# Two transfers instead of five for the sketch matrices, placed behind the first keys, and a new instruction sequence, in an attention and token-mixing kernel

## The chip, the cores and the metric

The kernel runs on one core of a Trainium2 chip. The metric is the device time of one execution in microseconds (us); the median of several runs counts. The core's engines run side by side, each through its own list of instructions: TensorE (PE, matrix products), VectorE (DVE), ScalarE (ACT), GpSimd (POOL) and SyncE (SP), which here only issues DMA transfers. An instruction waits until the data it reads is there and the buffer it writes is free.

## What is computed

```python
def phi(x):                                   # S1, S2: (8, 32)
    a = np.einsum('rd,bhsd->bhsr', S1, x)
    b = np.einsum('rd,bhsd->bhsr', S2, x)
    return np.einsum('bhsi,bhsj->bhsij', a, b).reshape(*x.shape[:-1], r * r)
q_p, k_p = phi(q), phi(k)                     # q, k, v: (4, 4, 1088, 32) float32
kv  = np.einsum('bhsf,bhsd->bhfd', k_p, v)
num = np.einsum('bhsf,bhfd->bhsd', q_p, kv)
den = np.einsum('bhsf,bhf->bhs', q_p, k_p.sum(axis=2))[..., None] + 1e-06
x = num / den                                 # then heads side by side: (4, 1088, 128)
...
theta = x @ w_theta
zr, zi = x * np.cos(theta), x * np.sin(theta)
y = einsum('ts,bsd->btd', w_tok_r, zr) + einsum('ts,bsd->btd', w_tok_i, zi)   # 1088 x 1088 each
u = x + y
out = u + np.maximum(u @ w_ch, 0.0)
```

S1, S2 and the weights are float64 in the inputs; q, k and v are float32. The denominator can be small, so sums over keys and queries are kept in several words of rounded parts.

## The kernel before

A 64-bit number arrives as two 32-bit words and is turned into float32 on the chip: ACT makes one word into a float, DVE shifts and joins the other. The kernel calls this path `wide`. It is taken for the sketch matrices S1, S2 (tile `st`, unpacked to `sp`), for the square weights (`w_sq`: w_theta and w_ch, unpacked to `w`) and for the 17 row blocks of the two token matrices (`w_tok`, raw tiles of class `zs`, unpacked into tiles of class `big`).

The stages are these.

1. For each of the four batches keys, queries and values are loaded (`load`, L677, 576 KB each, SP). ACT squares the keys and sums them (L702), PE sums over partitions, and DVE derives a rounding step (`key_step`, first DVE operation on `sm`) and rounds the keys into `hf`. PE forms the key sums from rounded part and remainder.
2. The sketch matrices are unpacked (ACT L471, then DVE shifts and masks, then ACT L483), scaled by a power of two (L495, then ACT L525 to L527) and split in rounded words (`s0`, first DVE operation `s<-sm`).
3. PE transposes keys, forms sketched features, and DVE multiplies them to outer products; PE sums these with the values (`kfeatures`).
4. Three "chains" (batch 0, batch 1, batches 2 and 3) carry the key sums through the sketch; DVE takes their norms (L918) and cuts them in words.
5. Queries get the same treatment (`query_scale` L1006, `query_slices`), then numerators and denominators (`levels`, L1071), theta, cosine and sine on ACT, and the products with x into tiles of class `zs`.
6. The token mix multiplies by the 17 row blocks (`mix_row`), for batches 0 and 1 directly, for batches 2 and 3 by a scheme of seven quarter products instead of eight (`winograd`). It needs sums and differences of quarter matrices; three sets of these are made by DMA transfers that add into their target (`aadd`, L1331, issued by POOL). Such adding transfers also join u = x + y for batches 0 and 1 (L398).
7. The channel product, ReLU, a transpose and the stores (L1286, SP).

No scheduler decides the order. Every piece of work is recorded as an operation with engine, buffers and a duration for planning; the list `ORDER` (1012 numbers) at the top of the file gives the order in which all operations are issued, for all engines together. `Layout.lay` walks that list, plans a start time for each operation from the durations and some constants (`START`: the time at which each engine begins; `ADD_FLY3`: the flight of an adding transfer), and with these picks which buffer of its class each tile gets. `Layout.issue` then emits the instructions in the list's order. Where the plan leaves a gap on PE, it puts in fill matmuls on a zero tile (`spin`, L435), whose result nobody reads. So on each engine the order is the list's; the planned times change only buffer numbers and the number of fills.

The helper lines L384 to L404 record almost every DVE, POOL and PE instruction, so that a line alone does not tell the operation; tile names do.

SP's queue begins with keys of batch 0, w_sq, the sketch transfers, keys of batch 1, queries of batch 0. The sketch transfers are made by `read_heads` (L452 to L457): S1 and S2 side by side, 32 partitions of 128 bytes, are read four times, once for each head's group of 32 partitions, two of them by ACT and two by SP; then SP reads S2 once more in another layout (8 partitions of 256 bytes, into columns 16 to 47 of `st`). A memset of `st` (L463) comes ahead of all, on DVE. On ACT the first Square of keys (L702) comes before the sketch unpack (L471).

Of the kernel before, what the change touches and what calls it, by code (L numbers as in the profile page):

```python
# [21 lines left out]
P = 128  # L22
# [4 lines left out]
TINY = 2.0**-60  # L27
UP = 256.0
ORDER = """
# [37 lines left out]
"""  # L67
WARM = 0
FILL = 5.0
# [13 lines left out]
UDMA = (True, True, False, False)  # L83
ADD_FLY = 2.85
ADD_FLY2 = 1.05 / 384
ADD_FLY3 = 1.6
QFIX = 2.006
NFIX = 1.002

# [16 lines left out]
class Layout:  # L106


    START = {"P": 1.3, "V": 0.8, "A": 1.0, "G": 1.3, "S": 0.9}
    ISSUE = 0.47  # L110
    LAT = {"P": 0.2, "V": 0.04, "A": 0.04, "G": 0.06, "S": 0.10}
    SAME = {"P": 0.0, "V": 0.035, "A": 0.035, "G": 0.05, "S": 0.0}
# [94 lines left out]
    def lay(self):  # L207
# [4 lines left out]
        slots = {c: [[0.0, None, i] for i in range(n)] for c, n in self.classes.items()}  # L212
        free = dict(self.START)
        channel = self.FIRST
# [105 lines left out]
def kernel(  # L320
# [12 lines left out]
    B, _, NC, H, D = q.shape  # L333
    S, DM = out.shape[1], out.shape[2]
    R = s_2.shape[0]
# [34 lines left out]
    op, buf = L.op, L.buf  # L370
# [4 lines left out]
    V, A, G, T, SY = nc.vector, nc.scalar, nc.gpsimd, nc.tensor, nc.sync  # L375

    def fixed(shape, dt, name):
        b = Buf(None, shape, dt, name)
        n = math.prod(shape) * WORD[dt]
        b.ap = view(const.tile([P, (n + 3) // 4], F32, tag=name, name=name), shape, dt)  # L380
        return b
# [4 lines left out]
    def ts(o, a, s1, op0, s2=None, op1=None, eng=None):  # L386
        kw = {} if op1 is None else {"op1": op1}
        (eng or V).tensor_scalar(out=o, in0=a, scalar1=s1, scalar2=s2, op0=op0, **kw)  # L388
# [59 lines left out]
    NS = 2 * R + D  # L448
    sp = fixed((2, NS), F32, "sp")
    wide = s_t.dtype != F32  # L450

    def read_heads(E, i0, i1):  # L452
        dst = st() if wide else sp()[:, 0]
        for i in range(i0, i1):
            E.dma_start(dst[i * D:(i + 1) * D, 0:2 * R], s_t.rearrange("d t r -> d (t r)"))
        if i1 == H:
            E.dma_start(dst[0:R, 2 * R:NS], s_2)  # L457

    if wide:
        st = fixed((NS,), I64, "st")  # L460
        y = fixed((NS,), I32, "sy")
        z = fixed((NS,), I32, "sz")
        op("V", 0.1, lambda: V.memset(st().bitcast(F32), 0.0), [st], [])  # L463
        op("A", 0.48 * 2, lambda: read_heads(A, 0, 2), [(st, 0)], [], fly=2.7)
        op("S", 0.5, lambda: read_heads(SY, 2, H), [(st, 1)], [], lk=3)

        def words():
            w = st().bitcast(I32).rearrange("p (n t) -> p n t", t=2)
            return w[:, :, 0], w[:, :, 1]

        op("A", 0.25, lambda: A.activation(sp()[:, 0], words()[1].bitcast(F32), AF.Prelu, scale=2.0**-112,  # L471
                                           alpha=-(2.0**32)), [(sp, 0)], [st])

        def unpack():
            wl = words()[0]
            x = sp()[:, 0].bitcast(I32)
            ts(x, x, 3, ALU.logical_shift_left)
            stt(x, wl, 29, x, ALU.logical_shift_right, ALU.bitwise_or)
            ts(y(), x, -(1 << 23), ALU.bitwise_and)
            ts(z(), wl, 0x1FFFFFFF, ALU.bitwise_and)  # L480

        op("V", 0.85, unpack, [(sp, 0), y, z], [st], lk=2)
        op("A", 0.25, lambda: A.activation(sp()[:, 1], z(), AF.Copy, scale=2.0**-52), [(sp, 1)], [z])  # L483
        vop(NS, lambda: tt(V, sp()[:, 1], sp()[:, 1], y().bitcast(F32), ALU.mult), [(sp, 1)], [y])
    else:
        op("V", 0.2, lambda: V.memset(sp(), 0.0), [sp], [])
        op("A", 0.4 * H + 0.4, lambda: read_heads(A, 0, H), [(sp, 0)], [], fly=2.0)

    def powers(mfn, m, n, name):

# [6 lines left out]
        def inv():  # L497
# [16 lines left out]
                                    op=ALU.max, apply_absolute_value=True), [m2], [(sp, 0)])  # L514
# [787 lines left out]
    def winograd():  # L1302
# [25 lines left out]
        def aadd(name, dst, x):  # L1328
            at("ac", name)
            for i in range(NF):  # L1330
                op("G", 1.05, lambda i=i: G.dma_start(dst[0](i), x[0](i), accum_op=ALU.add), [dst[1](i)], [x[1](i)],  # L1331
                   chan=ADD_FLY3)

# [170 lines left out]
```

## Time and profile before

| what | value |
|---|---|
| time, median of 3 runs (lowest, highest) | 223.31 us (223.21, 223.4) |
| profiled execution: time, span | 223.25 us, 221.4 us |
| granted clock of PE | 1.00 in all stretches read |
| DMA moved | 40.19 MB, mean 182 GB/s |
| DMA share, 10 to 50 us | 1.02 to 1.04 |
| L404 PE, `ps<-big,zs` (token mix) | x366, 102.4 us busy |
| L435 PE, `ps<-idle` (fills) | x40, 10.9 us busy |

The span runs from the first to the last instruction that the profile records; 1.8 us of the execution lie around it. "Busy" is the time in which an engine works on an instruction; an engine that is not the bottleneck may be idle at no cost. The chain of waits follows the work that ended last back to the start, at each step to whatever released it. A DMA share of 1.0 means that all 16 DMA engines are occupied. `[2.29 <-DMA big<-k_l]` behind an instruction says that its engine stood idle for 2.29 us before it and what ended that. DVE's first five instructions of the sketch unpack start at 7.12, 7.33, 7.58, 7.68 and 7.77 us, and its first rounding of the sketch (`s<-sm`) at 12.33 us.

### The profile page before, as it was taken

To read this page: it belongs to the slowest core of one execution; us is meant where nothing else is said; L and a number is where in the kernel's file an instruction comes from. 1 tells how busy PE (TensorE), PEld (TensorE's weight loads), DVE (VectorE), ACT (ScalarE), POOL (GpSimd) and SP (SyncE) were. 2 spreads that over 40 slices of the span, in tenths; PEclk is the share of its full clock that TensorE was granted. 3 is DMA by queue.
4 is the path that set the end of the run, shared out by engine and by line. 5 is a ranking of instruction groups with operands and counts; after the bars stand their busy time and mean duration, and the time that the engine had idled before them with its cause. 6 is when DMAs were issued, how large, how long until landed. Compare 5 with 4: busy or idle time off the path is not lost.

```text
span 221.4 us, 5134 instructions
## 1 busy us (share of the span) xinstructions
PE 212.4 (96%) x2067; PEld 160.3 (72%) x2067; DVE 167.2 (76%) x360; ACT 115.5 (52%) x237; POOL 47.4 (21%) x81
## 2 busy tenths in 40 slices
PE   7998999899998999999999999999999999999993
PEld 3796888697765756686666685778787888688782
DVE  2999889999999999999999949961798551043741
ACT  4889489988798889769640232586820000000000
POOL 1365751104000000100400090000552337101000
PEclk9999999999999999999999999999999999999999
DMA  6999999993509016948950089020498199983373
GB/s 184 367 410 341 393 411 375 414 360 150 204 16 366 25 42 242 385 154 302 338 103 0 0 134 170 3 39 1 69 179 152 33 171 158 169 122 56 47 116 57
DMA packets 27047, 40.19 MB, mean 182 GB/s; under 512 B 18320, under 2 KB 19344, under 8 KB 24848
## 3 DMA queue, kind: packets, MB, share of 16 engines
q1 hardware_dynamic: 22176, 30.29, 40.2%
q0 software_dynamic: 4752, 9.57, 24.2%
q8 instruction: 16, 0.26, 0.4%
q14 instruction: 7, 0.06, 0.1%
q10 hardware_dynamic: 96, 0.01, 0.0%
HBM read 28.07 MB, written 2.23 MB: 137 GB/s over the span
## 4 chain that ended last, share of the span: by engine, by line
PE 78%; DVE 12%; DMA 5%; SPq 2%; issue 1%; ACT 1%; POOL 0%; DVEq 0%; POOLq 0%
PE ps L404 68%; PE ps L435 4%; DMA zs<-big 3%; DVE g L384 2%; DVE lv L384 2%; PE ps L795 2%; DMA out<-g 2%; PE ps L1158 2%; SPq L1286 2%; PE ps L1191 1%; DVE big L384 1%; PE ps L1038 1%; DVE sm L384 1%; DVE big L388 1%; DVE big L391 1%
## 5 line engine op out<-in xcount | busy, mean ns | idle before, releaser
L404 PE MATMUL ps<-big,zs 128*128 128x384 f32 (+4 forms) x366 | 102.4, 426 | 0.6 <-DVE big L384 0.4
L404 PEld LDWEIGHTS ps<-big,zs 128*128 128x128 f32 x366 | 65.5, 190 | 27.2 <-issue 1.3
L1270 ACT COPY g<-ps 128x384 f32<-128x384 f32 (+1 forms) x6 | 2.6, 464 | 51.2 <-PE ps L404 51.2
L652 ACT ACTIVATE big<-zs 128x1088 int32<-128x1088 uint32 (+1 forms) x18 | 21.2, 1182 | 1.2 <-DMA zs<-w_tok 1.2
L384 DVE CUSTOM_DVE_ANT_0 big<-big,big 128x2176 uint16<-128x2176 uint16 x17 | 21.7, 1285 | 0.1
L650 ACT ACTIVATE big<-zs 128x1088 f32<-128x1088 f32 x17 | 20.6, 1220 | 1.6 <-DMA zs<-w_tok 0.8
L1331 POOL DMA_DIRECT2D big<-zs x8 | 7.9, 1026 | 34.1 <-DVE g L391 23.7
L391 DVE SCALAR_TENSOR_TENSOR big<-ps,even,big 128x256 f32<-128x256 f32 (+1 forms) x10 | 4.9, 498 | 13.5 <-PE ps L404 13.4
L384 DVE TENSOR_TENSOR zs<-ps,g 128x768 f32<-128x768 f32 (+2 forms) x20 | 12.4, 628 | 2.9 <-PE ps L1191 1.4
L404 PE MATMUL ps<-mf,big 128*128 128x96 f32 x72 | 14.3, 295 | 0.0
L398 POOL DMA_DIRECT2D g<-big x6 | 7.1, 1589 | 30.2 <-ACT g L1270 30.2
L404 PE MATMUL ps<-big,big 128*32 128x32 f32 (+2 forms) x320 | 12.9, 219 | 0.0
L388 DVE TENSOR_SCALAR big<-big 128x1088 int32<-128x1088 int32 x17 | 11.9, 720 | 0.4 <-ACT big L650 0.4
L435 PE MATMUL ps<-idle 128*128 128x384 bf16 x40 | 10.9, 406 | 1.3 <-POOL idle L437 1.3
L404 PEld LDWEIGHTS <-hf 128*32 128x32 bf16 (+1 forms) x252 | 10.5, 99 | 2.2 <-issue 1.2
L404 PEld LDWEIGHTS ps<-big,big 128*32 128x32 f32 (+1 forms) x320 | 9.9, 117 | 2.7 <-issue 0.9
L388 POOL TENSOR_SCALAR mf<-mv 128x32 f32<-128x32 f16 (+1 forms) x3 | 1.0, 341 | 49.7 <-DVE mv L388 49.7
L404 PE MATMUL ps<-w,big 128*128 128x128 f32 x76 | 10.9, 279 | 0.8 <-ACT g L1298 0.8
L404 PEld LDWEIGHTS ps<-w,big 128*128 128x128 f32 x76 | 9.9, 191 | 2.0 <-ACT g L1298 1.2
L384 DVE TENSOR_TENSOR g<-lv 128x768 f32<-128x768 f32 x12 | 11.1, 949 | 0.2
L404 PEld LDWEIGHTS ps<-mf,big 128*128 128x128 f32 x72 | 10.9, 191 | 0.1
L404 PE MATMUL ps<-mv,hf 128*128 128x96 f16 x108 | 10.6, 206 | 0.3 <-ACT big L810 0.3
(199 smaller groups left out, 396.2 us busy)
## 6 DMA issues: line engine op xcount, KB each, us to landing
zs<-w_tok SPq DMA_DIRECT2D x17, 1088.0 KB, 6.6
big<-k_l SPq DMA_DIRECT2D x7, 576.0 KB, 6.6
big<-q_l SPq DMA_DIRECT2D x4, 576.0 KB, 12.9
big<-v_l SPq DMA_DIRECT2D x4, 576.0 KB, 13.7
big<-big POOLq DMA_DIRECT2D x8, 272.0 KB, 5.8
big<-zs POOLq DMA_DIRECT2D x8, 272.0 KB, 4.4
zs<-big POOLq DMA_DIRECT2D x8, 272.0 KB, 5.5
big<-hf POOLq DMA_DIRECT2D x3, 576.0 KB, 10.2
```

Source lines behind the costliest of these rows:

```text
L384: eng.tensor_tensor(out=o, in0=a, in1=b, op=f)
L388: (eng or V).tensor_scalar(out=o, in0=a, scalar1=s1, scalar2=s2, op0=op0, **kw)
L391: (eng or V).scalar_tensor_tensor(out=o, in0=a, scalar=s, in1=b, op0=op0, op1=op1)
L398: op("G", 1.05, lambda: G.dma_start(dst(), src(), accum_op=ALU.add), w, r, chan=chan)
L404: T.matmul(o, lhs, rhs, start=start, stop=stop, skip_group_check=True)
L435: T.matmul(nowhere(), idle()[:, 0:P], idle(), start=True, stop=True, skip_group_check=True)
L650: op("A", 0.22 + n * 0.0009, lambda: A.activation(dfn(), words_of(raw(), n)[1].bitcast(F32), AF.Prelu, scale=2.0**-112, alpha=-(2.0**32)), ...
L652: op("A", 0.22 + n * 0.0009, lambda: A.activation(stp(), words_of(raw(), n)[0].bitcast(U32), AF.Copy, scale=2.0**-29), [stp], [raw])
L795: T.transpose(tr()[:, i * P:(i + 1) * P], kx()[:, g * GC + i].rearrange("p h d -> p (h d)"), ident())
L1158: T.transpose(tr()[:, i * P:(i + 1) * P], qp()[:, i * H + 2 * n:i * H + 2 * n + 2].rearrange("p h i j -> p (h i j)"), ident())
L1286: SY.dma_start(out[b, t0 - o:t0 + w, f * SQ:(f + 1) * SQ].rearrange("(c j) i -> j c i", j=SQ), ot()[f * SQ:(f + 1) * SQ, :o + w].rearrange ...
L1331: op("G", 1.05, lambda i=i: G.dma_start(dst[0](i), x[0](i), accum_op=ALU.add), [dst[1](i)], [x[1](i)], chan=ADD_FLY3)
```

## The change

- The four transfers of S1 and S2 side by side become one, whose source is read four times over (`partition_broadcast`), into all 128 partitions. That transfer and the one of S2 are both issued by SP. ACT issues none. One operation of the list goes (1011 numbers).
- The whole of `ORDER` is replaced. In it the two sketch transfers stand right behind the keys of batch 0 on SP, and w_sq behind them; further down SP's loads differ in places. DVE begins with the memset of `st`. On ACT the sketch unpack (old L471) stands before the first Square of keys, on DVE the sketch unpack before the first key step, and the unpacking of w_sq follows later. The order on PE, DVE, ACT and POOL differs in many places up to the token mix and in some behind it. On POOL the last of the adding transfers (old L1331) now stands behind the last join (old L398) instead of before it.
- `START` begins each engine sooner in the plan, and `ADD_FLY3` goes from 1.6 to 1.9. Fills become 39, 13 of them ahead of the first transposes instead of 17.
- The branch for float32 sketch matrices is changed in the same way; these inputs do not take it.

```diff
 ORDER = """
-    0 1 10 11 36 12 3 13 4 5 54 48 108 14 39 58 49 55 51 15 102 59 96 109 56 16 19 60 139 143 61 62 63 64 65 66
...
+    0 1 35 12 5 13 10 11 107 14 53 15 16 18 54 108 57 55 101 19 58 20 47 48 59 17 3 4 60 61 62 63 64 65 66 38 67
...
-ADD_FLY3 = 1.6
+ADD_FLY3 = 1.9
...
-    START = {"P": 1.3, "V": 0.8, "A": 1.0, "G": 1.3, "S": 0.9}
+    START = {"P": 1.05, "V": 0.55, "A": 0.75, "G": 1.05, "S": 0.5}
...
-    def read_heads(E, i0, i1):
+    def read_small():
         dst = st() if wide else sp()[:, 0]
-        for i in range(i0, i1):
-            E.dma_start(dst[i * D:(i + 1) * D, 0:2 * R], s_t.rearrange("d t r -> d (t r)"))
-        if i1 == H:
-            E.dma_start(dst[0:R, 2 * R:NS], s_2)
+        SY.dma_start(dst[:, 0:2 * R], s_t.rearrange("d t r -> d (t r)").partition_broadcast(H))
+        SY.dma_start(dst[0:R, 2 * R:NS], s_2)
...
         op("V", 0.1, lambda: V.memset(st().bitcast(F32), 0.0), [st], [])
-        op("A", 0.48 * 2, lambda: read_heads(A, 0, 2), [(st, 0)], [], fly=2.7)
-        op("S", 0.5, lambda: read_heads(SY, 2, H), [(st, 1)], [], lk=3)
+        op("S", 0.25, read_small, [st], [], lk=3)
```

More of the change, by code (lines that the diff above doesn't have):

```diff
@@ L486 @@
         op("V", 0.2, lambda: V.memset(sp(), 0.0), [sp], [])
-        op("A", 0.4 * H + 0.4, lambda: read_heads(A, 0, H), [(sp, 0)], [], fly=2.0)
+        op("S", 0.25, read_small, [(sp, 0)], [], lk=3)
     def powers(mfn, m, n, name):
```

72 rows, old and new, of the table ORDER are left out of this document.

## The prediction

> **What bounds the kernel now.** I read the busy shares and the chain first, then the chain in order of time.
>
> ```profile
> PE 212.4 (96%) x2067; PEld 160.3 (72%) x2067; DVE 167.2 (76%) x360; ACT 115.5 (52%) x237; POOL 47.4 (21%) x81
> PE 78%; DVE 12%; DMA 5%; SPq 2%; issue 1%; ACT 1%; POOL 0%; DVEq 0%; POOLq 0%
> ...
> 75.55 22.41 PE ps L404 x147
> ...
> 185.16 6.20 DMA zs<-big
> 191.40 21.06 PE ps L404 x90
> ```
>
> TensorE (PE) sets the end. From 75.55 us it is never idle except at 191.40, so whatever makes PE reach that point sooner passes to the end, unless the accumulating DMAs of the last product (zs<-big) then come too late. Before 75 us the limit changes hands, which the busy time by stretch shows (columns: stretch, its length, busy us of PE, PEld, DVE, ACT, POOL, clock, DMA share, GB/s):
>
> ```profile
> 30.00:42.00 12.00, 10.60 (x174) 9.46 (x174) 11.62 (x30) 11.60 (x28) 4.28 (x10) 1.00 1.03 391
> 58.00:70.00 12.00, 11.24 (x152) 7.62 (x151) 11.63 (x20) 11.28 (x24) 0.00 (x0) 1.00 0.40 137
> 100.00:140.00 40.00, 40.00 (x235) 26.51 (x234) 36.22 (x55) 15.47 (x23) 8.87 (x10) 1.00 0.59 144
> ```
>
> At 30-42 and 58-70 us VectorE (DVE) is the fullest (11.62 and 11.63 of 12), ScalarE (ACT) close behind, and the chain runs through DVE there. So the early gain is counted on DVE: how late it is against the work that stands ahead of it. Its waits up to 76 us, whole:
>
> ```profile
> DVE sm L388 <- ACT big L702: 3.4, 1, 3.4
> DVE sm L918 <- PE ps L404: 0.9, 1, 0.9
> DVE halfpi L419 <- PEq L1494: 0.8, 1, 0.8
> DVE big L388 <- ACT lv L1071: 0.5, 1, 0.5
> DVE s L388 <- ACT sm L527: 0.2, 1, 0.2
> ```
>
> Only the 3.4, 0.9, 0.5 and 0.2 can be won. The 3.4 is the place of the change; the timeline there (start, duration, engine, line, what):
>
> ```profile
> 0.73 0.38 SPq L677 DMA_DIRECT2D big<-k_l  x1
> 1.16 0.42 SPq L649 DMA_DIRECT2D zs<-w_sq  x1
> 2.29 0.14 DVE L463 MEMSET st<- 128x96 f32 x1
> 2.46 0.81 SPq L455 DMA_DIRECT2D st<-s_t  x2
> 2.46 0.88 ACTq L455 DMA_DIRECT2D st<-s_t  x2
> 3.31 0.36 SPq L457 DMA_DIRECT2D st<-s  x1
> 3.71 0.36 SPq L677 DMA_DIRECT2D big<-k_l  x1
> 4.50 1.16 ACT L702 ACTIVATE big<-big 128x1152 f32<-128x1152 f32 x1 [2.29 <-DMA big<-k_l]
> 5.79 0.34 DVE L388 TENSOR_SCALAR sm<-sm 128x1 int32<-128x1 int32 x2 [3.36 <-ACT big L702]
> 5.99 0.23 ACT L471 ACTIVATE sp<-st 128x48 f32<-128x48 f32 x1
> ```
>
> The first keys land at 4.48, ACT squares them at once, and DVE, idle for 3.36 us, goes on at 5.79. The sketch unpack (L471 on ACT, then four DVE operations and the reduction, 7.12-7.93) stands behind that.
>
> **The change, part by part.** The sum is made against the profiled execution: 223.25 us, span 221.4 and 1.8 us around it. It lies 0.06 under the median 223.31, so I carry the difference over unchanged.
>
> *Five transfers become two, on SP only.* SP saves one issue of about 0.4, ACT two (0.88). ACT waited 2.29 for the keys afterwards, so its saving is worth nothing. The memset (0.14) leads DVE, inside the 3.36 wait: nothing. On SP the order is now k0, two sketch transfers, w_sq, k1, q0. At 0.4 an issue k1 leaves near 2.4 instead of 3.71, q0 near 2.8 instead of 4.50. The DMA engines are full from 10 to 50 us (share 1.03), so later loads come 1 to 1.5 us sooner. I price that at nothing and use it as the cover for the terms below; without it the loads would eat them.
>
> *The sketch ahead of the first keys.* ACT now does the sketch activation (L471) before the first Square (L702), and DVE's five unpacking operations stand ahead of the key step. Let the sketch land at T. The Square starts at T+0.25 (0.23 for L471 and 0.02), the key step 1.29 later (5.79-4.50). DVE has 1.85 of work ahead of it, 1.19 before: its lateness is T+0.25+1.29-1.85 = T-0.31, against 5.79-1.19 = 4.60. Break-even is T=4.91. T is not in the trace. Lower bound: right with the keys, 4.55. Upper: as late as the last piece now, 5.84. In between: the present pieces, issued at 2.46 to 3.31, land 0.19 to 0.71 behind w_sq (5.13), the load issued ahead of them; the same distance behind the keys gives 4.67 to 5.19. I take 4.85: -0.06. The scale chain behind the unpack starts some 2 us sooner, so the 0.2 wait on L527 goes too. Head: -0.3, bounds -0.6 and +0.7 (T=5.84: +0.93-0.23).
>
> [...]
>
> *The new sequence.* (a) At 25.34 DVE waits 0.86 for PE before the norms (L918). The new order puts 1.7 us of other DVE work ahead of it (a key remainder, a row shift, a rounding). That wait goes if the moved work is ready: its inputs are the loads that now come sooner. -0.7, bounds -0.86 and 0. (b) The 0.46 at 58.02 (DVE on ACT's L1071, itself on PE): PE is sooner, -0.2, bounds -0.46 and 0. (c) Work ahead of the last big DVE step before 70 us (g<-lv at 68.25), summed from the durations of this trace: 59.32 before, 59.55 after: +0.24. (d) New waits: a key-feature product now stands behind an ACT copy that by the same sums comes 0.35 late, and a query Square behind a load near 26.8; +0.2, bounds 0 and +0.7. (e) Fills: 13 spins (L435) lead instead of 17, 39 in all instead of 40. They run while PE has nothing else: nothing.
>
> *The last product.* PE's real work from 75 us on is the same and stands in nearly the same order. The accumulating row additions (L1331) are reordered on POOL. Now PE loses 0.27 at 191.40 (with the rows before it 0.8 of lateness builds up from 184 to 193). In the new order the last row addition stands behind the last join (L398) on POOL: from the end of the matmul group that the join needs, PE has 4 matmuls of 256 columns (0.43 apart) and 11 of 288 (0.485 apart), 7.1 us, until it needs that row. The way takes 0.2 (a reader starts 0.2 behind PE's next group, as at 198.08 and 198.28) + 0.48 (copy, L1270) + 0.29 (its end at 201.27 to the join at 201.56) + 0.86 (the join's issue) = 1.8, then the landing, 4.4 to 5.8 by the medians of the row additions: 6.2 to 7.6. So -0.8 (old lateness gone) to +0.5; I take 0. The constants START and ADD_FLY3 act only through the planner: fills and buffer numbers.
>
> Sum: -0.3-0.7-0.2+0.24+0.2 = -0.76: 222.5 us, span 220.7.
>
> **Rivals.**
> - *The gain is hidden.* ACT has 11.60 of 12 at 30-42 us and DMA is at its limit to 50 us. If ACT or a landing sets that stage, (a) is won and lost again, (b) stays: 0 to -0.2, 223.2. For it: ACT's busy time. Against: DVE stands in the chain there, and the loads come sooner.
> - *The final join blocks POOL.* The slower side. The join's own DMA shares the queue with the row addition, and joins landed in medians of 4.6 (four of 192 KB) and 7.0 us (two of 160 KB). With 7.0 for the row addition the way is 8.8, PE stands 1.7 longer, and -0.76+1.7 = +0.9: 224.2. It decides from a landing of 5.3 us on, and outweighs the gain from about 6.1. For it: POOL takes its instructions in order and L398 waited 12.36 for ACT here. Against: from 192 to 213 us the DMA share is 0.58, against 1.05 before.
> - *The sketch lands late.* 128 pieces of 128 bytes behind the keys, or a repeated source that goes slowly. At T=5.84, +0.7-0.7-0.2+0.24+0.2 = +0.24: 223.5; each 0.1 later adds 0.1, as both the Square and DVE stand behind it, so at 6.5 it is 224.1.
> - *The change doesn't do what it says*: the reading is neutral (T near 4.9) and all comes from the order. The time is then the forecast's, +0.06+0.2 at most: 222.8; it is no case of its own.
> - *Cold PE.* The 17 spins here start about 0.32 us apart up to 6.4 us and then near 0.165; with 13 they end near 5.5, before that step. The first nine key transposes (0.109 each) would then cost double, +1.0 on PE if nothing covered it: 222.5+1.0 = 223.5. Against: DVE, not PE, sets the pace there, and PE still spins after them. [...]
>
> **How the numbers follow.** Forecast, with its own range 221.6 (all low ends but the last product's: -0.6-0.86-0.46+0.24 = -1.7) to 222.9: 0.58. Hidden: 0.15. Final join: 0.14. Late sketch: 0.09. Cold PE: 0.04. The runs shown spread by 0.2 us, so I count 0.2% (0.45 us) as what a measurement can tell. Faster is the forecast, 0.58; within it is the hidden gain and a little of the late sketch and cold PE, 0.17; slower the rest, 0.25. The range for 8 in 10: low end, all low ends with the last product's -0.8, is 220.7; I take 220.8. The high end takes in the final join and half of what the late sketch reaches: 224.5.
>
> **What would show it.** Right: L471 first on ACT, starting before 5.0; DVE's wait for it ends there and the key step starts by 6.3; s (L388 after L527) at or before 12.0; no wait of 0.9 at L918; PE past 75.55's piece some 0.7 sooner. Wrong: a sketch landing after 5.3, DVE or ACT waits over 0.5 us on a load before 50 us, or PE waiting over 0.5 us for zs<-big past 190 us.

## The result, and the profile after

The changed kernel takes 222.31 us (median of 6 runs, 221.82 to 222.86) against 223.36 us (6 runs, 223.15 to 223.57): a ratio of 0.9953, 95% interval 0.9933 to 0.9972. The forecast was 222.5. In three later jobs, on chips where the kernel before took 223.5 to 223.7, it was faster still: 221.90, 221.35 and 221.85 us, ratios 0.9919 (0.9884 to 0.9954), 0.9905 (0.9872 to 0.9939) and 0.9912 (0.9878 to 0.9946). So it is faster by 1.0 to 2.1 us. Some executions of some kernels ran 2 to 5% longer at a lower granted clock (0.945 to 0.974 on the mean); the medians and ratios here leave those out. The profiled execution below is the slowest of the first six: 222.86 us, span 221.1.

Busy shares and the chain by engine:

```profile
PE 212.8 (96%) x2066; PEld 160.8 (73%) x2066; DVE 167.0 (76%) x360; ACT 114.9 (52%) x237; POOL 45.5 (21%) x81
PE 80%; DVE 5%; ACT 5%; SPq 3%; DMA 3%; issue 2%
```

DVE's share of the chain falls from 12 to 5%. By stretch (columns as in the prediction; the first row is the kernel before, whose other two rows stand there):

```profile
180.00:192.00 12.00, 11.71 (x51) 9.11 (x50) 3.25 (x7) 0.00 (x0) 5.62 (x7) 1.00 1.05 164
30.00:42.00 12.00, 11.01 (x157) 9.55 (x157) 10.36 (x25) 10.22 (x25) 4.00 (x8) 1.00 1.03 392
58.00:70.00 12.00, 12.00 (x194) 8.23 (x193) 11.19 (x21) 11.70 (x24) 0.00 (x0) 1.00 0.37 135
180.00:192.00 12.00, 12.00 (x52) 9.68 (x51) 3.32 (x8) 0.00 (x0) 5.47 (x7) 1.00 1.01 167
```

At 30-42 us DVE works 10.36 where it worked 11.62: something held it up, and in this execution the front of the kernel was no faster. At 180-192 us PE is busy all the time; before, it was busy for 11.71 of the 12 us. DVE's waits up to 76 us, from the same view as before:

```profile
DVE sp L388 <- ACT sp L468: 2.9, 1, 2.9
DVE sm L388 <- PE ps L404: 1.3, 1, 1.3
...
DVE sm L915 <- PE ps L404: 0.7, 1, 0.7
DVE big L388 <- ACT lv L1068: 0.6, 1, 0.6
```

The wait ahead of the norms (now L915), which was to go, is still 0.7, and one of 1.3 on PE is new. The reordered start itself did what was said (timeline, first sketch and key operations):

```profile
5.00 0.24 ACT L468 ACTIVATE sp<-st 128x48 f32<-128x48 f32 x1 [2.79 <-DMA st<-s]
5.15 1.15 ACT L699 ACTIVATE big<-big 128x1152 f32<-128x1152 f32 x1
...
6.42 0.34 DVE L388 TENSOR_SCALAR sm<-sm 128x1 int32<-128x1 int32 x2 [0.33 <-ACT big L699]
```

**How the profiles are compared.** From the query products of batch 2 on (the 37th matmul `ps<-mf,big`) PE hardly waits: 1.5 us in all in the profile of before, 0.8 in that of after. I cut each profile there: "front" is the time from the span's start to that matmul, "rest" from it to the span's end. "Issue" is PE's idle time up to 76 us that the view of waits puts down to nothing it knows. All in us, each from one profile:

| kernel | front | rest | issue |
|---|---|---|---|
| before | 94.41 | 127.0 | 1.0 |
| before_swap | 94.46 | 126.8 | 0.6 |
| before_early6 | 94.38 | 126.2 | 0.3 |
| headB_tailA | 94.98 | 125.9 | 0.8 |
| headB_again | 94.15 | 125.9 | 0.3 |
| after | 94.98 | 126.1 | 2.4 |
| after_again | 93.77 | 126.1 | 0.6 |
| after_third | 93.05 | 126.1 | 0.2 |
| after_fourth | 94.12 | 126.1 | 0.8 |
| headA_tailB | 94.96 | 127.6 | 1.7 |
| seqA_five | 94.28 | 125.9 | 0.9 |
| after_sketch_late | 96.06 | 126.3 | 1.4 |
| after_nofill | 95.86 | 126.7 | 0.4 |

The rest is 125.9 to 126.3 with the changed tail (but for after_nofill) and 127.0 or more with the old one. PE's own part of it, from the cut to the end of its last matmul, repeats to 0.01 us: 122.75 or 122.76 in eight of the nine profiles with the changed tail (123.00 in after_sketch_late), 124.24 before. What follows PE's last matmul, the last copies and stores, takes longer with the changed tail: 3.12 to 3.34 instead of 2.79, and 3.97 in after_nofill. So PE gains 1.5 us in the tail, and the span keeps about 1.0 of it. The front scatters by 1.9 us for one and the same changed front (the four runs called after, and headA_tailB).

### The profile page after: what moved, and what is told of

The parts are those of the page before. It is cut to its first block, busy times and chain, and to the rows that moved or that the text cites. A ratio compares the mean times of both kernels' runs of the same rounds, so it can differ in the third digit from the quotient of the medians.

```text
span 221.1 us, 5129 instructions
## 1 busy us (share of the span) xinstructions
PE 212.8 (96%) x2066; PEld 160.8 (73%) x2066; DVE 167.0 (76%) x360; ACT 114.9 (52%) x237; POOL 45.5 (21%) x81
## 4 chain that ended last, share of the span: by engine, by line
PE 80%; DVE 5%; ACT 5%; SPq 3%; DMA 3%; issue 2%
PE ps L404 73%; SPq L1283 3%; DMA big<-k_l 2%; PE ps L1188 2%; PE ps L1155 2%; PE ps L792 2%; ACT big L649 2%; PE ps L435 1%; DVE lv L384 1%; DVE g L384 1%; DMA out<-g 1%; PE ps L1035 1%; ACT big L699 1%; DVE big L391 1%; ACT big L1003 1%
## 5 line engine op out<-in xcount | busy, mean ns | idle before, releaser
L404 PE MATMUL ps<-big,big 128*32 128x32 f32 (+2 forms) x320 | 14.1, 220 | 0.2 <-issue 0.2
L1328 POOL DMA_DIRECT2D big<-zs x8 | 7.0, 1132 | 34.7 <-PE ps L404 29.4
L1328 POOL DMA_DIRECT2D big<-big x8 | 9.2, 1638 | 19.7 <-issue 19.7
L398 POOL DMA_DIRECT2D g<-big x6 | 7.8, 1433 | 23.4 <-ACT g L1267 23.4
L1295 ACT COPY g<-ps 128x128 f32<-128x128 f32 x2 | 0.5, 265 | 23.0 <-PE ps L1293 22.0
```

Of the source, the lines that this page charges most:

```text
L398: op("G", 1.05, lambda: G.dma_start(dst(), src(), accum_op=ALU.add), w, r, chan=chan)
L404: T.matmul(o, lhs, rhs, start=start, stop=stop, skip_group_check=True)
```

## Experiments

The query products that the expectation of after_third assigns to batch 1 are those of batch 2. Operation numbers are the numbers that stand in the list ORDER; the changed kernel's are lower by one from 14 on.

### Which half makes the gain

headA_tailB takes the changed kernel's first 545 operations (all up to the token mix) and the others in the order of before; headB_tailA the reverse.

```diff
+first = set(AFTER[:545])
+ORDER = AFTER[:545] + [x for x in BEFORE_RENUMBERED if x not in first]
```

> The changed kernel up to the token mix (its first 545 operations, the two transfers among them), then the rest in the order of before. Theory 1 (the prediction's): the gain is made ahead of 75 us, the rest is even; 222.3 to 222.6. Theory 2: the gain is made by the order of the row additions and the products behind 140 us, and the front is even or loses up to 0.6; 223.2 to 223.9.

> The kernel before up to the token mix (five transfers, its first 545 operations), then the rest in the changed kernel's order. Theory 1: no gain, 223.2 to 223.5, with PE at the 147 token-mix matmuls by 75.5. Theory 2: the whole gain, 222.2 to 222.6, and no PE wait for zs<-big near 191.

Measured: the changed head alone 223.11 us, ratio 0.9987 (0.9957 to 1.0017); the changed tail alone 222.45 us, 0.9940 (0.9912 to 0.9968), against 223.64 for before and 221.90 for the whole change in the same rounds. So theory 2 holds for the tail, and the head is not shown to be worth anything by itself.

> Front of before, tail of the changed kernel, again, in the same rounds as the changed kernel. If the whole gain is the tail: within 0.2 us of the changed kernel. If the changed front gains as the first job's medians say (222.45 against 221.9): 0.5 to 0.7 slower than the changed kernel.

Measured: 222.81 us, ratio 0.9958 (0.9929 to 0.9987), with 221.85 for the whole change (0.9912) and 223.69 for before. The changed front is worth 0.96 by these medians and 0.55 by the first job's; the intervals overlap. By the table's fronts it is 0.3 (mean of five 94.18, of five old ones 94.48). So a gain of the front is likely, and its size stays open.

### What in the tail

In the kernel before, the eight row additions of the last product leave like this (timeline of POOL):

```profile
178.59 1.78 POOL L1331 DMA_DIRECT2D zs<-big  x2 [1.49 <-PE ps L404]
183.22 0.86 POOL L1331 DMA_DIRECT2D zs<-big  x1 [2.86 <-PE ps L404]
184.62 3.53 POOL L1331 DMA_DIRECT2D zs<-big  x4 [0.54 <-DMA out<-g]
188.34 0.86 POOL L1331 DMA_DIRECT2D zs<-big  x1 [0.19 <-issue]
```

An addition overwrites its row of the difference matrix in place, and product 6 reads that row first. The third waits 2.86 us for PE. First I moved only the work behind: six groups of product 5 go ahead of the ones that wait.

```diff
-951 935 843 844 952 880 940 941 936 953 845 846 847 848 849 850 937 954
+951 935 843 844 845 846 847 848 849 850 952 880 940 941 936 953 937 954
```

> The kernel before with one edit: in the last products six matmul groups that need no row addition (product 5, 2.9 us of work) stand ahead of the group of four that waits for one (in the profile 0.28 us at 189.46 and 0.54 at 191.41, with the matmul behind each wait slow by 0.1 of that). Theory A, those waits are the tail's whole gain: 0.8 us faster than before, 222.5 to 222.7 against 223.3 to 223.5, no PE wait for zs<-big. Theory B, the waits only move to the next group that needs a row: 0 to -0.2. Theory C, the changed tail gains by its last stores too: -0.8 here and 0.2 more in the changed kernel.

Measured: 222.93 us, ratio 0.9966 (0.9947 to 0.9986), before at 223.49. The rest falls by only 0.2, and PE's wait for a row behind 150 us shows where it went:

```profile
PE ps L404 <- DMA zs<-big: 0.2, 1, 0.2
```

The wait has moved to the next rows: counted from the cut, PE is 0.82 us ahead of before at 194.8 and only 0.22 ahead at 198.6. By this profile that is theory B. The times do not decide it: the interval of the ratio is -0.3 to -1.2 us, which leaves out B's 0 to -0.2 and takes in A's -0.8. Then I moved what the additions wait for: product 6 reads rows 2 to 6 in one go.

```diff
-873 966 518 519 520 933 911 912 913 888 889 914 915 874 929 521 925 949 875 876 824 828 829 877 878 916
+873 874 875 876 877 878 966 518 519 520 933 911 912 913 888 889 914 915 929 521 925 949 824 828 829 916
```

> The kernel before with one edit: the second half of product 6 (its 288-column part) reads rows 2 to 6 of the difference matrix in one go, 0.5 to 4 us sooner, as in the changed kernel, and not spread among product 3. The row additions overwrite those rows in place and can only be issued once product 6 has read them: in the profile of before the third waits until 183.23 (2.86 us idle on POOL) and the eighth leaves at 188.35; in the changed kernel seven have left by 184.01. Theory A, that is the tail's gain: additions issued by about 185, no PE wait for zs<-big, 0.8 faster than before. Theory B, the consumers' order matters too: 0.3 to 0.5. Theory C, neither: 0.

Measured: 222.71 us, ratio 0.9948 (0.9918 to 0.9979), before at 223.69; the rest is 126.2. POOL now issues seven additions in one run:

```profile
178.56 6.21 POOL L1331 DMA_DIRECT2D zs<-big  x7 [1.49 <-PE ps L404]
188.31 0.86 POOL L1331 DMA_DIRECT2D zs<-big  x1 [3.55 <-PE ps L404]
```

and no PE wait for zs<-big is left. Five moved groups give 0.8 of the 0.9 to 1.1 that the whole changed tail gives in the profiles, and by the medians as much as the whole tail in the same rounds (0.98, headB_again 0.88). So theory A holds. By the times alone this run and before_swap cannot be told apart; the profiles separate them. PE's own part falls here by the same 0.82 as in the changed tail up to 193 us; the other 0.66 of the changed tail comes in the last channel products, where one of two waits of PE for ACT (0.4 us, L1298) is gone, and the last stores take half of it or more back. The changed kernel's own lines answer to it, and to the rival of the final join:

```profile
179.32 6.22 POOL L1328 DMA_DIRECT2D zs<-big  x7 [0.97 <-PE ps L404]
194.89 0.86 POOL L398 DMA_DIRECT2D g<-big  x1 [9.35 <-ACT g L1267]
195.42 1.21 POOL L1328 DMA_DIRECT2D zs<-big  x1
```

The last addition does stand behind the join, leaves at 195.42, and nobody waits for it: PE reads that row at 200.85, 5.4 us later, without a gap (it landed at 199.88). The join's issue cost 0.53 there, not the 0.86 in the prediction's way.

### Is the front's scatter chance?

> The changed kernel once more, for a second profile. In the first profile (222.86 us, the slowest of six runs) PE stood 0.94 us at 34.29 and 0.86 at 21.57 in the middle of a group of equal matmuls, with nothing that the profile shows to wait for, and reached the piece of 147 token-mix matmuls at 76.12, later than before (75.55). Theory 1, those standstills are chance: here the one at 34.29 is missing, that piece starts at 75.2 to 75.6, and the time is 221.8 to 222.3. Theory 2, they belong to the new sequence: both are there again and the piece starts at 76.1.

> The changed kernel again, in the same rounds as the three others. If the tail gives 0.8 to 1.0 and the front is even on average: 222.3 to 222.5 where before has 223.3 to 223.5. If the front gains 0.5 besides: 221.8 to 222.0. The front differs by up to 1.2 us from profile to profile (query products of batch 1 at 94.99 and 93.78), all of it made ahead of 53 us.

> The changed kernel, as the measure for the three others in the same rounds: 221.6 to 222.3.

The changed kernel unaltered. Measured: 221.90, 221.35 and 221.85 us, the ratios given above. PE reaches the place of the cut at 93.77, 93.05 and 94.12. The first profile's two standstills (timeline, then PE's waits up to 76 us: total, count, longest):

```profile
33.98 0.32 PE L404 MATMUL ps<-mf,big 128*128 128x96 f32 x1
35.24 0.35 PE L404 MATMUL ps<-mf,big 128*128 128x96 f32 x1 [0.94 <-issue]
```

```profile
PE ps L404 <- issue: 2.2, 4, 0.9
```

Two matmuls of one kind, nothing to wait for, 0.94 us between. In the fastest profile (after_third) the same view says:

```profile
PE ps L404 <- issue: 0.2, 1, 0.2
```

and the waits of DVE there have no L915 among them. The one on PE that is left, at 35.69 us:

```profile
DVE sm L388 <- PE ps L404: 0.2, 1, 0.2
```

So the standstills are chance in size, theory 1. They are not chance in place: over all profiles they come at PE's matmul records 220, 346 or 347, 471 to 474, 599 and 852 (347 and 474 in the profile of before, 220, 346, 471, 599 and 852 in that of after), which are, to within two records, multiples of 126.5 apart. In these two profiles the record behind one starts 1.35 to 1.56 us after the end of a 16 KB packet on a DMA queue that the page calls "instruction" (q8). Each has 16 such packets, which took 0.89 to 1.06 us up to 50 us; PE's 4134 matmuls and weight loads of before are 258 for each packet, and 126.5 matmuls with their weight loads are 253. So I take it that PE stood for its instructions. No view names the engine that the queue serves, and no run changed their supply by itself, so that is not shown. Subtracting "issue" from "front" gives 92.6, 93.2, 92.9, 93.3 and 93.3 for the changed front (spread 0.7 instead of 1.9) and 93.4 to 94.2 for the old one.

If the standstills are that, they cost up to 2.4 us in one execution (after), with a DMA share of 0.99 from 10 to 50 us.

### Fills

```diff
-FILL = 5.0
+FILL = 0.0
```

> The changed kernel without the 12 fills that the plan puts into gaps (27 of 39 fill matmuls stay). Prediction: fills cost nothing, so no change, 222.0 to 222.4. Theory F, PE stands in the front because its instructions come late: the standstills in the middle of equal matmuls sit at fixed counts from the start (before matmul records 346, 599 and 852 in all traces so far, 253 apart) and 1.3 to 1.6 us behind a 16 KB packet of the instruction queue. Without the fills they stay at the same counts, and so fall at places of the program that are up to 12 matmuls further on. Theory G, they belong to places of the program (a semaphore or buffer): the counts shift by up to 12.

It takes out 11 of the 39; 28 stay. Measured: 222.95 us, ratio 0.9971 (0.9947 to 0.9995), against 221.35 for the changed kernel in the same rounds: 1.6 slower. So in these rounds the fills were no cost but worth 1.6 us, which the prediction had not priced. The granted clock of the profiled execution (224.36 us, the slowest of twelve), in 40 slices of the span:

```profile
PEclk9998599999999999999999999999999999999999
```

The granted clock is 0.5 from 20.22 us for 6.83 us (0.52 on the mean of 20 to 25 us, 0.80 of 25 to 30). In ten of the twelve executions the mean granted clock is 0.982 to 0.991, and they take 223.2 us in the median; the two with 1.0 take 222.07 and 222.18, and the changed kernel's have 0.997 to 1.0. So by these two, as an estimate, the fall of the clock makes up about 1.1 of the 1.6 us; the rest stays open. PE was busy for 2.79 of the 3.42 us before the fall, against all 3.42 in the changed kernel's first profile, where six fills stand from 18.81 to 19.62 and the granted clock is 1.00. What makes the clock fall is not shown. On the standstills: the one at record 346 stays (0.43), as theory F has it; the other long gaps of this profile (records 279 and 664, 0.62 and 0.64) are put down to ACT, so one place supports F and no more.

### Transfers

seqA_five is the changed sequence with the old five transfers; seqB_two the old sequence and constants with the two.

```diff
 seqA_five
-op("S", 0.25, read_small, [st], [], lk=3)
+op("A", 0.48 * 2, lambda: read_heads(A, 0, 2), [(st, 0)], [], fly=2.7)
+op("S", 0.5, lambda: read_heads(SY, 2, H), [(st, 1)], [], lk=3)
```

> The changed kernel's sequence and constants, with the five transfers of before (two issued by ACT, three by SP) in the place of the two. If the number of transfers is worth nothing (prediction: nothing but SP's issue time), 222.2 to 222.5, the sketch activation starting within 0.3 of 5.00. If ACT's own row lets its part slip in among the keys' packets, the activation starts by 4.5 only if SP's part does too. If the five cost the head, it starts after 5.4 and the time is 222.6 to 222.9.

> The sequence and constants of before with the two transfers of the change, still behind w_sq on SP. Prediction: the number of transfers is worth nothing, 223.2 to 223.5 as before, the scaled sketch's first rounding at 12.0 to 13.4. Rival: fewer issues on ACT and SP let the later loads leave sooner, 222.8 to 223.0.

seqA_five: 222.55 us, ratio 0.9949 (0.9920 to 0.9979), 0.65 above the changed kernel in the same rounds (0.9884 to 0.9954; the intervals overlap). Its sketch activation starts at 5.68, not at 4.80 to 5.11 as in the five profiles with the changed front: the last piece lands some 0.7 later, although ACT's two leave at 0.98. The start fits the third expectation, that the five cost the head; the time lies just under its 222.6, and the profile's front (94.28) is no later than the changed kernel's mean, so a cost in time is not shown. ACT's two transfers have a DMA queue of their own, the expectation's "row" (in the profile of before 96 packets on q10, from 3.99 to 4.89 us, with those of w_sq on q1 among them), but the second expectation's activation by 4.5 did not come. The number of transfers did something else: SP does not issue the queries of batch 0 before the first keys have landed (4.68, issue at 4.70):

```profile
SPq L677 <- DMA big<-k_l: 1.4, 1, 1.4
```

In the five profiles of the old front, too, they leave 0.01 to 0.02 us behind that landing (4.48 to 4.67); with the two transfers they leave at 3.28 to 3.30.

seqB_two: 224.16 us, ratio 1.0029 (1.0003 to 1.0055): not faster, rather slower, and why stays open; its profile shows half the granted clock from 22.0 to 35.7 us and cannot be compared with the others. That the two transfers are worth something only where they stand ahead of the sketch's first use fits both runs, and is not shown.

### The sketch behind the keys again

```diff
-0 1 35 12 5 13 10 11 107 14 53 15 16 18 54 108 57 55 101 19 58 20 47 48 59 17
+0 1 35 12 5 13 10 11 107 53 14 54 108 57 55 101 58 15 16 18 19 20 47 48 59 17
```

> The changed kernel with the sketch unpack behind the first keys again: ACT does the first Square and then the sketch activation, DVE the key step and rounding and then the unpack; the plan puts in 12 more fills. Prediction: the order is worth 0.06 at T=4.85 and the scale chain's earlier start about 0.2, so 0.1 to 0.4 slower than the changed kernel, the first rounding of the scaled sketch 0.1 to 0.4 later. If the front's time is set elsewhere (instruction supply, loads): no difference beyond 0.2.

Measured: 223.04 us, ratio 0.9978 (0.9954 to 1.0003), 1.2 above the changed kernel in the same rounds, more than the 0.1 to 0.4 expected. The first rounding of the scaled sketch came at 12.69, against 11.94 to 12.67 in the five profiles with the changed front: 0.45 above their mean. The rest of the 1.2 the profile does not tie to the order: PE stood 1.50 us at record 220 (put down to ACT, L1038, and 1.4 us behind the end of a 16 KB packet on the queue called "instruction") and 1.17 at 599. The plan's 6 added fills (45 instead of 39; the expectation says 12) move what stands at those records, so this run does not separate the order from the standstills.

## Why the prediction was right, and where it was wrong

- **Direction** was right, and the size in the first job: -0.8 forecast, -1.05 measured. In the later jobs it was -1.7 to -2.1, more than twice the forecast, though inside the stated range of 220.8 to 224.5. That the first number came so near is luck in part: the forecast put the whole gain ahead of 75 us and nothing in the tail, and the runs show about 1.0 in the tail and less than forecast, 0.3 by the table, in the front.
- **The last product, "So -0.8 (old lateness gone) to +0.5; I take 0"**: mis-sized. The tail measured -0.9 to -1.1 (rest 127.0 to 125.9-126.1), the largest term of all, and 0.8 of it is this term. The mechanism stood in the text as its lower bound; what I missed is that the additions wait for product 6's reads, which the new order puts together. I looked at what stands behind the additions on POOL and not at what they wait for on PE. The rival of the final join did not happen: the last addition landed 4.5 us after its issue.
- **Head, -0.3**: the sketch landed near 4.98 for a forecast T of 4.85, and the key step came at 6.42, after the 6.3 I had set; the arithmetic holds (T-0.31 gives 4.67 of lateness, measured 6.42-1.85 = 4.57). Yet the scaled sketch's first rounding came at 12.24 on average over five profiles, against 13.04 over five of the old front: -0.8. I had compared with 12.33 from a single profile, the earliest of those five.
- **"I price that at nothing"** (the loads that leave sooner): here, most likely, is that difference (read from the order on ACT, not tried by itself). The queries of batch 0 leave at 3.3 instead of 4.5 to 4.7. In the profile before, ACT's first query Square found them just landed; in the four other profiles of the old front it waited 0.9 to 1.2. One of these (headB_again), and the changed kernel:

```profile
10.01 1.16 ACT L1006 ACTIVATE big<-big 128x1152 f32<-128x1152 f32 x1 [0.90 <-DMA big<-q_l]
```

```profile
9.37 1.17 ACT L1003 ACTIVATE big<-big 128x1152 f32<-128x1152 f32 x1
```

- **(a), -0.7 at L918**, the largest term of the sum: not borne out. The wait that it would win seems to be chance itself. Of the five profiles of the old front only two have it (0.9 before, 0.3 in headB_tailA), and of the five of the changed front also two (0.7 in the first, 1.2 in headA_tailB). These four are the ones in which PE stood longest at record 346 or 347, some 4 us ahead of it (0.21 to 1.10 us, 0.76 before; 0.19 or less in the other six). A new wait of DVE on PE, 0.2 to 1.3 us near 37 us, is in all five profiles of the changed front and in none of the old.
- **(b), -0.2**: wrong, the wait on ACT's levels is 0.6 in all four profiles of the changed kernel. **(c)** and **(d)** can't be told apart from the scatter.
- **(e), fills "nothing"**: right for this change, where 39 stand instead of 40 and the granted clock is 1.00 in both profiles, and not in general: without 11 of them the kernel was 1.6 us slower.
- **SP's issues**: the transfer with the repeated source took 0.71 us to issue, not 0.4, so k1 left at 2.83 instead of 2.4 and the gain in issues is smaller than assumed. Most of the queries' gain is not issue time: with the five transfers SP waited for the first keys to land.
- **Cold PE** came true in part: in the first profile the first three key transposes, from 5.47 us, start 0.215 apart instead of 0.109, but DVE waits for PE nowhere before 25 us there.
- **The front together**: -0.76 forecast. Without "issue" it is -0.8 (five-profile means 93.0 and 93.9), though not by (a); that standstills take part of it back, 1.1 on average in the changed front and 0.6 in the old one, is worked out from profiles and was not tried by itself.

## What to carry to other kernels

Ask of every stalled transfer what it waits for, and then whether the readers in its way can be put together: five moved matmul groups were worth 0.8 us here. Take the baseline from several profiles, because a transfer that lands "just in time" in one is 0.9 to 1.2 us late in the next, and a wait worth 0.9 us in one is missing in the next. Where an engine stands with nothing to wait for while the DMA engines are full (share 0.99 to 1.03 here), look for standstills at equal numbers of instructions (253 here) before blaming an order.

## What the runs showed of the hardware that I had not expected

Beside the kernel's own loads, 16 packets of 16 KB run on a DMA queue called "instruction", one for each 258 of PE's matmuls and weight loads in the profile of before. Up to 50 us one took 0.89 to 1.06 us in the profiles of before and after, and at the standstills 1.35 to 1.56 us passed from its end to the next matmul. Standstills at these places left PE idle for 0.2 to 2.4 us in the same kernel, with a DMA share of 0.99 from 10 to 50 us in the first of its profiles; without them the fronts of its profiles differ by 0.7 us instead of 1.9. And 11 fill matmuls, 0.16 to 0.18 us apart and with no reader, were worth 1.6 us by the medians; in the profile without them the granted clock is 0.5 for 6.83 us, after a stretch of 3.42 us in which PE was busy for 2.79.
